# Which scores VectorE copies out of PSUM, and which two ScalarE takes as its second pair

## The chip, the core and the metric

The kernel runs on one core of a Trainium2 chip. The metric is the device time of one execution in microseconds. Engines are named as the profile names them: PE is TensorE's matmul, PEld its weight load, DVE is VectorE, ACT is ScalarE, POOL is GpSimd, SP is SyncE, which issues the DMAs.

## The reference

Two branches read the same x of 2048 rows and 512 columns, and a gate mixes them by row. Cut to what matters:

```python
# A: attention, 32 heads of 16 columns
q, k, v = split(x @ wqkv)                       # each (32, 2048, 16)
p = softmax(q @ k.T * 16**-0.5)                 # (32, 2048, 2048)
a = (p @ v) @ wo
# B: token-mixing MLP over the rows
h = layernorm(x)
b = (gelu(h.T @ w1 + b1) @ w2 + b2).T
g = sigmoid((x * gate_w).sum(-1))
out = g * a + (1 - g) * b
```

The attention has 32 x 2048 x 2048 exponentials, 134 million in all. Everything is float32; the kernel multiplies with high and low parts.

## The kernel before, in words

A first stage (to about 277 us) projects V, K and half of the queries, and runs the first layer of the MLP. Then come 128 attention *phases*, and beside them, in matmuls that use the half of PE's rows that a score leaves free, the second layer of the MLP, the late queries and the output projection ("beside" in the code, tile `dn`). A last stage finishes the output projection.

Four phases make a *group*: one pair of heads (head 0 and head 1) over half of the queries, so 32 groups. A phase computes 16 *scores*, numbered 0 to 15. A score is one matmul (L1067) of 128 keys by 512 queries, it fills one PSUM bank, and its contraction lies in the upper or the lower 64 rows of PE, by its head. In the phases with 14 matmuls beside, scores 0 to 13 are of one head, and 14 and 15, which have no matmul beside them, of one head each and run at the same time. In phases with 12 beside (16 in the middle, for late queries, and the last 16, for the output projection) 12 and 13 are of one head each too. Their order is then 12, 13, 15, 14.

Each score's exponential is taken in one of three ways:

- SINGLE: six scores, each exponentiated by ACT straight from its bank (L1093), into a tile `p`.
- TWO: two pairs of scores in neighbouring banks, a pair in one instruction of 1024 columns (L1031).
- EVAC: six scores that DVE copies (L1089) into an SBUF tile `pe`; ACT exponentiates all six at the end of the phase in one instruction of 3072 columns (L1102).

SINGLE and TWO are multiplied with V in their own phase (list TURNS), EVAC in the next one (list HELD), which the code calls held. The products (L963) are 32 columns wide and run four at a time, in four strips of PE; a pair in TURNS or HELD supplies all four. They add into one bank, `av`. In a group's first phase the held products belong to the group before and go to `av`, and the phase's own go to the bank of score 10, shown as `t`. At the end of a phase DVE adds the bank to the group's sum `ot` (L985). Which of the four quarters of the bank (two heads in column halves, two query blocks in row halves) were written decides whether that is one add of 128x512, one of 128x256, or one of 128x256 and one of 64x256.

Eight banks hold all this: one for `dn`, seven that change their use. The list `share` gives the seven banks in the order of use; scores 0 to 6 take them in that order, 7, 8 and 9 the first three again, and 10 to 15 and `av` the rest. A score must wait until the score that held its bank before was exponentiated or copied; a pair of banks is one tile (names t), released as one, and a single bank in the later part of a phase is named u.

On each engine the order is the order of the code. On DVE, work that `amid` or `between` lists for a phase stands at the last but one score, and work of `later` behind the copies.

Of the kernel before, what the change touches and what calls it, by code (L numbers as in the profile page):

```python
# [60 lines left out]
def gated_mix(ctx: ExitStack, tc: tile.TileContext, a_x, a_wqkv, a_wo, b_w1, b_b1, b_w2, b_b2, gate_w, out):  # L61
# [364 lines left out]
    with tc.tile_pool(name="gl", bufs=2, side="right") as gl:  # L426
# [74 lines left out]
        for f0, cs in order.items():  # L501
            n = min(NB, F - f0) // P
# [78 lines left out]
    PHASES, NSC, BANKS = 4, 16, 7  # L581
# [295 lines left out]
    for t in range(NS):  # L877
        at = put(second_layer(t), at, [14] * 3)
        if queries:
            b, n = queries.pop(0)  # L880
# [34 lines left out]

    token, mark = (out_pool.tile([1, 1], F32, name=name, bufs=1) for name in ("token", "mark"))

    EVAC = 1, 3, 5, 9, 14, 15
    SINGLE = 0, 2, 4, 6, 7, 8
    TWO = (10, 11), (12, 13)  # L920
    TURNS = [(0, 2), (4, 6), (7, 8), *TWO]
    HELD = [(1, 3), (5, 9), (14, 15)]

    def shares(n):

        for one in range(0, BANKS, 2):
            lows = [k for k in range(one)][::2] + [k for k in range(one + 1, BANKS)][::2]
            for third in lows:
                if n in (third, third + 1):
                    first, second = (low for low in lows if low != third)  # L930
                    return [first, first + 1, one, second, second + 1, 2 * third + 1 - n, n]


    def regions():
        return tc.tile_pool(name="ps_s", bufs=1, space=PSUM, reuse_waits="tile")
# [54 lines left out]
    with tc.manual_schedule(engines=engines):  # L990
        held, fence, turn, spare = [], None, 0, 0
        landed.clear()

        for p in range(LAST + 1):
# [22 lines left out]
            in_turn = list(range(n_b)) + ([14, 15] if n_b == NSC - 2 else [12, 13, 15, 14])  # L1017
            qbs = {}
            for a, b in TURNS + HELD:
                if head[a] == head[b]:  # L1020
# [3 lines left out]
                    qbs[zero], qbs[one] = turn, 1 - turn  # L1024
                    turn = 1 - turn

            def exps(n):
                pt = ptp.tile([P, 2, NB], F32, name="p2", bufs=len(TWO))
                where = [share[(j - BANKS) % BANKS] for j in (n - 1, n)]
                low = min(where)  # L1030
                pairs_done.append(nc.scalar.activation(pt, twos[low, low + 1], AF.Exp, scale=SCALE))  # L1031
                for j, k in zip((n - 1, n), where):
                    units[j] = *units[j][:3], pt[:, k - low, :]

            pairs_done = []
            evac = evp.tile([P, len(EVAC), NB], F32, name="pe")
            units = {}
            share = shares(spare)
# [3 lines left out]
            for n in in_turn:  # L1042
                i, qb = head[n], qbs[n]
                c = at[i][qb]
                at[i][qb] += 1
                if n < TWO[0][0]:
                    if n >= BANKS:
                        ones[share[n - BANKS]] = psum.tile([P, NB], F32, name=f"s{share[n - BANKS]}")
                    s = ones[share[n % BANKS]]
                else:  # L1050
                    if n == TWO[0][0]:
                        pool.__exit__(None, None, None)
                        pool = regions()
                        psum = pool.__enter__()
                        twos = {}
                        for low in range(BANKS):
                            if low == share[1]:
                                av = psum.tile([P, NB], F32, name="av")
                            elif low in (share[0], share[2]):
                                twos[low] = psum.tile([P, NB], F32, name=f"u{low}")  # L1060
                            elif low not in twos:
                                two = psum.tile([P, 2, NB], F32, name=f"t{low}")
                                twos[low], twos[low + 1] = two[:, 0, :], two[:, 1, :]
                                twos[low, low + 1] = two
                    s = twos[share[2 if n == NSC - 1 else (n - BANKS) % BANKS]]
                rows_i = slice(i * HALF, i * HALF + ROWS)
                nc.tensor.matmul(  # L1067
                    s,
                    kt[grp][rows_i, c * P : (c + 1) * P],
                    qt[grp][rows_i, qb * NB : (qb + 1) * NB],  # L1070
                    start=True,
                    stop=True,
                )
                if n < n_b:
                    ps, a, b, begin, last, done = beside[n]
                    mm = nc.tensor.matmul(ps, a[half], b[half], start=begin and not second, stop=last and bool(second))  # L1076
                    if n == 0 and fence is not None:
                        tc.add_manual_dep(mm.ins, fence.ins.name, SYNC, reason=REASON)
                    if n == n_b - 1:
                        fence = nc.gpsimd.memset(token, 0.0)  # L1080
                        tc.add_manual_dep(fence.ins, mm.ins.name, SYNC, reason=REASON)
                if n == in_turn[-2]:
                    if n_b and second and beside[-1][-1] in between:
                        between[beside[-1][-1]]()
                    for what, *args in amid.get(p, ()):
                        what(*args)
                if n in EVAC:
                    pt = evac[:, EVAC.index(n), :]
                    nc.vector.tensor_copy(pt, s)  # L1089
                    units[n] = i, c, qb, pt  # L1090
                elif n in SINGLE:
                    pt = ptp.tile([P, NB], F32, name="p1", bufs=len(SINGLE))
                    one = nc.scalar.activation(pt, s, AF.Exp, scale=SCALE)  # L1093
                    if n == SINGLE[-1] and p:
                        tc.add_manual_dep(one.ins, earlier.ins.name, SYNC, reason=EARLY)
                    units[n] = i, c, qb, pt
                else:
                    units[n] = i, c, qb, None
                    if n in (TWO[0][1], TWO[1][1]):
                        exps(n)  # L1100
            for x in ([evac] if p < LAST else [evac[:, :2, :], evac[:, 2:, :]]):
                done = nc.scalar.activation(x, x, AF.Exp, scale=SCALE)  # L1102
            tc.add_manual_dep(done.ins, pairs_done[0].ins.name, SYNC, reason=EARLY)
# [15 lines left out]
                what(*args)  # L1119

            turns, now_held = ([tuple(units[n] for n in pair) for pair in pairs] for pairs in (TURNS, HELD))
            spare = share[1]
            if ph == 0:
                if held:
                    apply_v(av, grp - 1, held, final=True)
                    spare = share[3]
# [103 lines left out]
    with tc.If(far_off != 0):  # L1230
        with (
# [6 lines left out]
            for b in range(ND):  # L1238
                with tc.For_i(0, P // DH, 1) as hi:
# [11 lines left out]
                    for t in range(NS):  # L1251
                        s = ps_s.tile([P, S], F32, name="s")
# [58 lines left out]
```

## Time and profile before

| | us |
|---|---|
| median of 3 runs | 1265.53 |
| lowest, highest | 1265.07, 1266.18 |
| the profiled execution | 1265.31 |
| its span from first to last instruction | 1263.5 |
| mean granted PE clock | 0.999 of full |

Read the profile by stage: a phase repeats 128 times, so a hundredth of a microsecond in each is 1.3 us in all. In the rows of the order of time, the first number is the start and the second the duration, from the start of the first to the end of the last where several equal instructions are merged (xcount). A bracket at a row's end tells how long the engine was idle before it, and what ended that. Neighbouring instructions of ACT and of DVE overlap in these rows: one starts before the other has ended.

### The profile page before, as it was taken

The numbers are of one execution on the slowest core, as the hardware profiler recorded it, in microseconds if no ns is written. First come the engines' busy times: TensorE is split into PE (matmuls) and PEld (weight loads), VectorE is DVE, ScalarE is ACT, GpSimd is POOL, SyncE is SP. The second block draws the span as 40 slices with busy tenths as digits, with TensorE's granted clock in tenths as the row PEclk, the third lists the DMA queues.
The fourth block names the chain that finished last, engine by engine and source line by source line (L and its number), as shares of the span: only waits on it lengthen the run. The fifth ranks groups of instructions, "written<-read, shape, count | busy, mean of one in ns | idle before, by whom it ended". The sixth has DMA issues, their size and how long they took to land.

```text
span 1263.5 us, 32833 instructions
## 1 busy us (share of the span) xinstructions
PE 1254.8 (99%) x13342; PEld 829.2 (66%) x13342; DVE 856.7 (68%) x1562; ACT 1069.0 (85%) x1405; POOL 198.6 (16%) x316
## 2 busy tenths in 40 slices
PE   9999999999999999999999999999999999999998
PEld 7888888875666666666666666666666666666656
DVE  5675453178767676767677677776777677678883
ACT  4443343269999999999999999999999999999990
POOL 0220444461010101010110101111111111000000
PEclk9999999999999999999999999999999999999999
DMA  4799443244744444544344433444543443366611
GB/s 134 251 340 329 143 122 106 81 127 110 214 121 104 90 102 85 158 86 97 77 105 94 99 90 83 91 87 81 113 101 73 90 100 60 56 166 175 151 60 70
DMA packets 100556, 152.32 MB, mean 121 GB/s; under 512 B 17109, under 2 KB 56171, under 8 KB 96300
## 3 DMA queue, kind: packets, MB, share of 16 engines
q1 hardware_dynamic: 99820, 149.08, 46.0%
q8 instruction: 107, 1.75, 0.6%
q10 hardware_dynamic: 576, 1.05, 0.2%
q14 instruction: 53, 0.43, 0.1%
HBM read 105.39 MB, written 44.68 MB: 119 GB/s over the span
## 4 chain that ended last, share of the span: by engine, by line
PE 96%; DVE 2%; ACT 1%; issue 0%; DVEq 0%
PE av L963 31%; PE s L1067 21%; PE acc L424 12%; PE t L1067 9%; PE acc L75 8%; PE t L963 5%; PE dn L1076 3%; PE u L1067 3%; PE pa L1162 2%; DVE pe L1089 1%; PE acc L199 1%; PE acc L268 0%; DVE ot L985 0%; PE acc L245 0%; ACT p L1093 0%; ACT pe L1102 0%
## 5 line engine op out<-in xcount | busy, mean ns | idle before, releaser
L1093 ACT ACTIVATE p<-s 128x512 f32<-128x512 f32 x768 | 411.9, 789 | 0.1
L1102 ACT ACTIVATE pe<-pe 128x3072 f32<-128x3072 f32 x129 | 380.9, 2954 | 0.0
L1067 PE MATMUL s<-qs,ks 64*128 64x512 f32 x1280 | 329.8, 400 | 0.6 <-ACT p L1093 0.6
L1089 DVE COPY pe<-s 128x512 f32<-128x512 f32 x512 | 323.6, 685 | 5.5 <-PE s L1067 1.5
L1067 PEld LDWEIGHTS s<-qs,ks 64*128 64x128 f32 x1280 | 225.7, 184 | 92.7 <-issue 52.3
L1031 ACT ACTIVATE p<-t 128x1024 f32<-128x1024 f32 x256 | 278.7, 1267 | 0.0
L963 PE MATMUL av<-p,v 128*32 128x256 f32 x3880 | 227.2, 379 | 0.0
L1089 DVE COPY pe<-u 128x512 f32<-128x512 f32 x256 | 164.8, 685 | 67.1 <-PE u L1067 67.1
L963 PE MATMUL av<-pe,v 128*32 128x256 f32 x3072 | 192.5, 383 | 0.0
L985 DVE TENSOR_TENSOR ot<-av,ot 128x512 f32<-128x512 f32 (+2 forms) x160 | 93.0, 582 | 140.9 <-PE av L963 139.6
L68 POOL TENSOR_TENSOR w_lo<-w_raw,w_hi 128x512 fp32r<-128x512 f32 (+1 forms) x128 | 153.0, 1202 | 196.8 <-ACT w_hi L67 99.9
L1076 PE MATMUL dn<-u_lo,w_hi 64*128 64x512 f32 x448 | 181.0, 404 | 0.0
L1076 PE MATMUL dn<-u_hi,w_hi 64*128 64x512 f32 x448 | 180.7, 403 | 0.0
L963 PEld LDWEIGHTS av<-p,v 128*32 128x32 f32 x3880 | 126.0, 110 | 83.3 <-ACT p L1093 0.2
L1076 PE MATMUL dn<-u_hi,w_lo 64*128 64x512 f32 x448 | 180.6, 403 | 0.0
L1067 PE MATMUL t<-qs,ks 64*128 64x512 f32 x512 | 142.5, 413 | 0.0
L963 PEld LDWEIGHTS av<-pe,v 128*32 128x32 f32 x3072 | 86.8, 109 | 80.7 <-ACT p L1093 35.7
L1080 POOL MEMSET token<- 1x1 f32 x128 | 11.3, 88 | 742.7 <-PE dn L1076 679.4
L67 ACT CAST w_hi<-w_raw 128x512 fp32r<-128x512 f32 (+1 forms) x67 | 38.0, 569 | 82.7 <-PE acc L424 63.1
L1067 PEld LDWEIGHTS t<-qs,ks 64*128 64x128 f32 x512 | 73.2, 184 | 50.8 <-ACT p L1093 48.6
L424 PE MATMUL acc<-h_hi,w_hi 128*128 128x512 f32 x224 | 87.9, 392 | 0.0
L424 PE MATMUL acc<-h_hi,w_lo 128*128 128x512 f32 x224 | 87.9, 392 | 0.0
(171 smaller groups left out, 1615.8 us busy)
## 6 DMA issues: line engine op xcount, KB each, us to landing
w_raw<-in_B_w_dram SPq DMA_DIRECT2D x96, 256.0 KB
ks<-kp SPq DMA_DIRECT2D x192, 128.0 KB
qs<-qp SPq DMA_DIRECT2D x256, 64.0 KB
kp<-pc SPq DMA_DIRECT2D x16, 512.0 KB
qp<-pc SPq DMA_DIRECT2D x8, 768.0 KB
qp<-row SPq DMA_DIRECT2D x24, 256.0 KB
v<-v SPq DMA_DIRECT2D x4, 1088.0 KB
x<-in_A_x_dram SPq DMA_DIRECT2D x16, 256.0 KB
```

The costliest lines, as they stand in the source:

```text
L67: copy(hi, src)
L68: return sub(lo, src, hi.bitcast(F32), ALU.subtract)
L75: nc.tensor.matmul(ps, a, b, start=start and n == 0, stop=stop and n == last)
L424: nc.tensor.matmul(p, a, b, start=first and k == 0, stop=last and k == 2)
L963: mm = nc.tensor.matmul(av[32 * j : 32 * (j + 1), i * QC : (i + 1) * QC], vb[b][:, v_at : v_at + 32], pt[:, h * QC : (h + 1) * QC], start= ...
L985: latest["add"] = nc.vector.tensor_tensor(x, y, x, ALU.add)
L1031: pairs_done.append(nc.scalar.activation(pt, twos[low, low + 1], AF.Exp, scale=SCALE))
L1067: nc.tensor.matmul(s, kt[grp][rows_i, c * P : (c + 1) * P], qt[grp][rows_i, qb * NB : (qb + 1) * NB], start=True, stop=True,)
L1076: mm = nc.tensor.matmul(ps, a[half], b[half], start=begin and not second, stop=last and bool(second))
L1089: nc.vector.tensor_copy(pt, s)
L1093: one = nc.scalar.activation(pt, s, AF.Exp, scale=SCALE)
L1102: done = nc.scalar.activation(x, x, AF.Exp, scale=SCALE)
```

## The change

DVE copies scores 8, 12 and 13 in place of 9, 14 and 15; score 9 becomes a single in place of 8; ACT's second pair is 14 and 15 in place of 12 and 13. So `av` takes the bank that scores 2 and 9 used, 14 and 15 the neighbouring banks of 7 and 8, and 12 and 13 get single banks. The lists TURNS and HELD follow.

```diff
-    EVAC = 1, 3, 5, 9, 14, 15
-    SINGLE = 0, 2, 4, 6, 7, 8
-    TWO = (10, 11), (12, 13)
-    TURNS = [(0, 2), (4, 6), (7, 8), *TWO]
-    HELD = [(1, 3), (5, 9), (14, 15)]
+    EVAC = 1, 3, 5, 8, 12, 13
+    SINGLE = 0, 2, 4, 6, 7, 9
+    TWO = (10, 11), (14, 15)
+    TURNS = [(0, 2), (4, 6), (7, 9), *TWO]
+    HELD = [(1, 3), (5, 8), (12, 13)]
...
-                            if low == share[1]:
+                            if low == share[2]:
                                 av = psum.tile([P, NB], F32, name="av")
-                            elif low in (share[0], share[2]):
+                            elif low in share[5:]:
                                 twos[low] = psum.tile([P, NB], F32, name=f"u{low}")
...
-                    s = twos[share[2 if n == NSC - 1 else (n - BANKS) % BANKS]]
+                    s = twos[share[(n - BANKS) % BANKS]]
...
-                    if n in (TWO[0][1], TWO[1][1]):
-                        exps(n)
+                    if n == TWO[0][1]:
+                        exps(*TWO[0])
+                    elif n == in_turn[-1]:
+                        exps(*TWO[1])
...
-            spare = share[1]
+            spare = share[2]
```

On PE, the last scores of a phase with 14 matmuls beside, before: the tile t is the pair 12 and 13, and the two u are 14 and 15; behind a row stands the engine on which it waits.

```order
L1067 MATMUL t_8628<-qs,ks 128x512 [waits DVE_49,Activation_49]
L1076 MATMUL dn<-u_hi,w_hi 128x512
L1067 MATMUL t_8628<-qs,ks 128x512
L1076 MATMUL dn<-u_lo,w_hi 128x512
L1067 MATMUL u_8629<-qs,ks 128x512 [waits Activation_49]
L1067 MATMUL u_8627<-qs,ks 128x512 [waits DVE_49]
L963 MATMUL av<-pe,v_113 32x256 [waits Activation_49]
```

The same place after:

```order
L1067 MATMUL u_8634<-qs,ks 128x512 [waits DVE_49]
L1076 MATMUL dn<-u_hi,w_hi 128x512
L1067 MATMUL u_8633<-qs,ks 128x512 [waits Activation_49]
L1076 MATMUL dn<-u_lo,w_hi 128x512
L1067 MATMUL t_8636<-qs,ks 128x512 [waits DVE_49,Activation_49]
L1067 MATMUL t_8636<-qs,ks 128x512
L963 MATMUL av<-pe,v_113 32x256 [waits Activation_49]
```

The pair now comes last, and its first matmul waits both for DVE's copy of score 8 and for ACT's single of score 7; scores 12 and 13 wait for one engine each.

On DVE, from the end of a group's first phase to the copies of its second, before: the first two adds are of the held products, the third of the phase's own (t), then come the copies.

```order
L985 TENSOR_TENSOR ot<-av,ot 128x256
L985 TENSOR_TENSOR ot<-av,ot 64x256
L985 TENSOR_TENSOR ot<-t_8631,ot 128x256
L1089 COPY pe<-s_8711 128x512
L1089 COPY pe<-s_8712 128x512
L1089 COPY pe<-s_8715 128x512
L1089 COPY pe<-s_8751 128x512
```

The same place after:

```order
L985 TENSOR_TENSOR ot<-av,ot 128x256
L985 TENSOR_TENSOR ot<-av,ot 64x256
L985 TENSOR_TENSOR ot<-t_8637,ot 128x256
L985 TENSOR_TENSOR ot<-t_8637,ot 64x256
L1089 COPY pe<-s_8718 128x512
L1089 COPY pe<-s_8719 128x512
L1089 COPY pe<-s_8722 128x512
L1089 COPY pe<-s_8753 128x512
```

A second add of the phase's own products, 64x256, now stands ahead of the copies. In groups that follow a phase with 14 matmuls beside, the 64x256 add of the held products is gone in return.

More of the change, by code (lines that the diff above doesn't have):

```diff
@@ L1025, in gated_mix, with exps @@
                     turn = 1 - turn
-            def exps(n):
+            def exps(a, b):
                 pt = ptp.tile([P, 2, NB], F32, name="p2", bufs=len(TWO))
-                where = [share[(j - BANKS) % BANKS] for j in (n - 1, n)]
+                where = [share[(j - BANKS) % BANKS] for j in (a, b)]
                 low = min(where)
                 pairs_done.append(nc.scalar.activation(pt, twos[low, low + 1], AF.Exp, scale=SCALE))
-                for j, k in zip((n - 1, n), where):
+                for j, k in zip((a, b), where):
                     units[j] = *units[j][:3], pt[:, k - low, :]
```

## The prediction

> **What bounds the kernel now.** I read the page first, then the waits, then the order of time engine by engine through one group of four attention phases. The page says PE 99% and puts nearly the whole chain on PE:
>
> ```profile
> span 1263.5 us, 32833 instructions
> PE 1254.8 (99%) x13342; PEld 829.2 (66%) x13342; DVE 856.7 (68%) x1562; ACT 1069.0 (85%) x1405; POOL 198.6 (16%) x316
> PE 96%; DVE 2%; ACT 1%; issue 0%; DVEq 0%
> ```
>
> The 85% of ACT is a mean over stages. The 128 attention phases run from its first exponential at 278.1 us to its last at 1227.4, and there ACT has no idle time; behind its rows stand the busy times of an ordinary group and of one of the last four (PE, PEld, DVE, ACT, POOL):
>
> ```profile
> L1093 ACT ACTIVATE p<-s x768: 579/801/871, 278.1 to 1224.2; 128x512 f32<-128x512 f32 x192
> L1102 ACT ACTIVATE pe<-pe x129: 1177/3001/3020, 283.0 to 1227.4; 128x3072 f32<-128x3072 f32 x127, 128x1024 f32<-128x1024 f32 x1, 128x2048 f32<-128x2048 f32 x1
> ...
> 604.90:634.60 29.70, 29.69 (x376) 18.04 (x372) 21.94 (x40) 29.70 (x37) 2.17 (x6) 1.00 0.41 92
> 1109.40:1139.30 29.90, 29.79 (x374) 18.19 (x370) 23.98 (x45) 29.90 (x37) 0.88 (x5) 1.00 0.70 177
> ```
>
> PE and ACT are both full, so the order of time must tell which sets the pace. ACT, in order: six singles (scores exponentiated straight from PSUM, L1093), two pairs (L1031), the big exponential of the six copied scores (L1102), the next singles:
>
> ```profile
> 602.79 3.00 ACT L1102 ACTIVATE pe<-pe 128x3072 f32<-128x3072 f32 x1
> 605.49 3.24 ACT L1093 ACTIVATE p<-s 128x512 f32<-128x512 f32 x6
> 608.37 2.19 ACT L1031 ACTIVATE p<-t 128x1024 f32<-128x1024 f32 x2
> 610.21 3.00 ACT L1102 ACTIVATE pe<-pe 128x3072 f32<-128x3072 f32 x1
> 612.90 3.24 ACT L1093 ACTIVATE p<-s 128x512 f32<-128x512 f32 x6
> ```
>
> Each row begins before the one ahead of it has ended: the singles at 605.49, the big exponential ahead at 605.79, an overlap of 0.30 us. So starts say little; I read the ends: 605.79, 608.73 (+2.94), 610.56 (+1.83), 613.21 (+2.65), together 7.42. Compare a place where the big exponential had started late and the overlap was small:
>
> ```profile
> 862.73 2.77 ACT L1102 ACTIVATE pe<-pe 128x3072 f32<-128x3072 f32 x1
> 865.40 3.02 ACT L1093 ACTIVATE p<-s 128x512 f32<-128x512 f32 x6
> 868.26 1.99 ACT L1031 ACTIVATE p<-t 128x1024 f32<-128x1024 f32 x2
> 870.07 2.84 ACT L1102 ACTIVATE pe<-pe 128x3072 f32<-128x3072 f32 x1
> ```
>
> Here the overlap is 0.10 (865.50 less 865.40), and the ends still stand +2.92, +1.83 and +2.66 apart: 7.41. So ACT's work, counted from end to end, takes 7.42 us a phase whether its instructions start early or late, and a start may come 0.20 us later than it does now (0.30 less 0.10) before an end moves. That is the cushion of this kernel.
>
> PE is tied to it. PE's weight loads: the phase's first score, its last two scores, the first product with V, the next phase's first score:
>
> ```profile
> 604.95 0.18 PEld L1067 LDWEIGHTS s<-qs,ks 64*128 64x128 f32 x1 [0.41 <-issue]
> 608.29 0.19 PEld L1067 LDWEIGHTS u<-qs,ks 64*128 64x128 f32 x2 [0.19 <-ACT p L1093]
> 608.78 1.02 PEld L963 LDWEIGHTS av<-pe,v 128*32 128x32 f32 x24 [0.30 <-ACT p L1093]
> 612.37 0.18 PEld L1067 LDWEIGHTS s<-qs,ks 64*128 64x128 f32 x1 [0.41 <-issue]
> 634.63 0.18 PEld L1067 LDWEIGHTS s<-qs,ks 64*128 64x128 f32 x1 [0.41 <-issue]
> ```
>
> The products start at 608.78, 0.05 after the last single ended (608.73), because av takes that single's bank. From there to the next phase is 3.59 us of products. So a phase is 7.42, the group 604.95 to 634.63 is 29.68, and ACT's ends set both.
>
> **The change part by part.**
>
> *The wait ahead of the big exponential goes.* Now DVE copies scores 14 and 15 last:
>
> ```profile
> 605.72 2.52 DVE L1089 COPY pe<-s 128x512 f32<-128x512 f32 x4
> 608.83 1.29 DVE L1089 COPY pe<-u 128x512 f32<-128x512 f32 x2 [0.58 <-PE u L1067]
> ```
>
> They end at 610.12 and the exponential starts at 610.21, 1.84 after the first pair; at 868.26, where nothing held it, it took 1.81. So 0.03 us a phase of waiting, 128 x 0.03 = 3.8 us if it counted. With the copies of 12 and 13 following that of 8 at 0.61 us each (2.52 over four, less the last one's tail), six copies end near 609.5, and that wait is over. I cost the gain at nothing: an earlier start only adds to an overlap of 0.30 that is already larger than the 0.10 ACT needs. Bounds: 0 and -3.8 us.
>
> *The second pair now waits for the last two scores.* Those matmuls start with the load at 608.29 and take about 0.5 (the row at 1120.50 below), so they are there by 608.8; the second pair starts 0.92 after 608.37 (half of 1.84), at 609.29. Margin 0.5 us: nothing. The last products use this pair last of 64 matmuls, over 2 us later. av moves to the bank of score 9, again the phase's last single, so its release stays at 608.73. Scores 14 and 15 now need both the single of 7 (the wait in the row at 608.29 today) and DVE's fourth copy, which is of score 8 instead of 9: the same place in DVE's order, ended at 608.24. Nothing.
>
> *The sums' adds move.* Which quarters of av were written decides how DVE adds them (L985). The scores on two heads were 14 and 15, held over; now they are in TURNS, so in all groups the first phase's own products fill three quarters, not two, and need a 128x256 and a 64x256 add. Today that is so in the last four groups alone:
>
> ```profile
> L985 DVE TENSOR_TENSOR ot<-av,ot x160: 402/690/693, 284.1 to 1231.4; 128x512 f32<-128x512 f32 x95, 128x256 f32<-128x256 f32 x34, 64x256 f32<-64x256 f32 x31
> L985 DVE TENSOR_TENSOR ot<-t,ot x35: 423/425/427, 315.9 to 1206.9; 128x256 f32<-128x256 f32 x31, 64x256 f32<-64x256 f32 x4
> ```
>
> The 4 becomes 31 (27 more); in return 64x256 adds of the held products fall away in the middle of a phase, where DVE waits for PE anyway. The new adds stand right ahead of the second phase's copies. What that does is seen in the last four groups (DVE, then PE's loads, a last-scores matmul, and ACT):
>
> ```profile
> 1117.07 0.87 DVE L985 TENSOR_TENSOR ot<-t,ot 128x256 f32<-128x256 f32 x2 [1.33 <-issue]
> 1117.96 2.48 DVE L1089 COPY pe<-s 128x512 f32<-128x512 f32 x4
> 1121.04 1.29 DVE L1089 COPY pe<-u 128x512 f32<-128x512 f32 x2 [0.59 <-PE u L1067]
> ...
> 1109.45 0.18 PEld L1067 LDWEIGHTS s<-qs,ks 64*128 64x128 f32 x1 [0.41 <-issue]
> 1116.87 0.18 PEld L1067 LDWEIGHTS s<-qs,ks 64*128 64x128 f32 x1 [0.41 <-issue]
> 1120.50 0.19 PEld L1067 LDWEIGHTS u<-qs,ks 64*128 64x128 f32 x2 [0.32 <-DVE pe L1089]
> 1124.52 0.18 PEld L1067 LDWEIGHTS s<-qs,ks 64*128 64x128 f32 x1 [0.41 <-issue]
> 1131.91 0.18 PEld L1067 LDWEIGHTS s<-qs,ks 64*128 64x128 f32 x1 [0.41 <-issue]
> 1139.26 0.18 PEld L1067 LDWEIGHTS s<-qs,ks 64*128 64x128 f32 x1 [0.41 <-issue]
> ...
> 1120.50 0.50 PE L1067 MATMUL u<-qs,ks 64*128 64x512 f32 x2
> ...
> 1121.19 1.29 ACT L1031 ACTIVATE p<-t 128x1024 f32<-128x1024 f32 x1
> 1122.42 2.77 ACT L1102 ACTIVATE pe<-pe 128x3072 f32<-128x3072 f32 x1
> ```
>
> The copies begin 1.09 after the phase's first score, against 0.77 (605.72 less 604.95). The fourth ends at 1120.44, and only then (1120.50) can the last scores be loaded; the phase lasts 1116.87 to 1124.52, 7.65 us, 0.23 more than 7.42. So in 27 more groups PE comes 0.23 late to the third phase's first score. ACT's single then starts 0.23 later; the cushion takes 0.20. I cost 0.03 x 27 = +0.8 us. The cushion must be refilled in the three other phases: PE, when ACT does not hold it, takes 7.39 and 7.35 (1124.52, 1131.91, 1139.26) against ACT's 7.42, and slightly less once the fourth copy need not wait for score 9 (2.48 against 2.52): near 0.07 a phase, 0.2 in three. Just enough. Bounds: 0, if the refill is ample; 0.13 a group, 3.5 us, if such a group becomes what the last four are now (29.81, from 1109.45 to 1139.26, against 29.68). I take 0.03, since those four pay for something the change removes, the next point.
>
> *The last four groups.* There the late last scores also delay their copies (1121.04) and with them the big exponential: 1122.42, 1.23 after its pair at 1121.19, against 0.92. After the change copies 12 and 13 do not come behind the last scores, and the pair's scores are there at 1121.00, before 1121.19. These groups fall from 29.81 to the others' 29.68 + 0.03: 4 x -0.10 = -0.4 us.
>
> Sum: +0.8 - 0.4 = +0.4 us on the profiled execution's 1265.31, which lies 0.2 under the median of 1265.53; on the median, **1265.9 us**.
>
> **The rivals.**
>
> *Slower: the cushion does not hold.* Mechanism: the added 64x256 add makes the third phase's first score late. If groups come out as the last four now, 27 x 0.13 = 3.5 us, 1269.0; if nothing is absorbed, 27 x 0.23 = 6.2 us, 1271.7. It decides from 0.11 us a group on (2.5 + 0.4 over 27). For it: the refill is barely enough. Against it: at 862.73 the overlap fell to 0.10 and ACT's ends kept their distance. The Trainium skill (ScalarE: Activation LUTs, What ACT_TABLE_LOAD costs) says that ACTIVATEs back to back overlap by about 93 ns, which would leave no cushion and make it the 1271.7; the trace agrees with 0.10 as the least overlap, but shows 0.30 as the usual one.
>
> *Faster: ACT's pace is that of its starts.* Singles start 0.48 apart (2.88 over six), and the big exponential's 0.03 of wait per phase would then be real: -3.8 us, 1261.7. Against it: the ends' distance is the same with and without waits, and PE's products go by an end. The Trainium skill (Perfetto Trace Analysis, Optimizing Scalar/DVE Operations) gives about 51 ns per ScalarE instruction on PSUM and 93 on SBUF; with the 0.833 ns an element of its ScalarE page that is an estimate of 7.32 us a phase, so that ACT would have idle time to give; the starts agree with it, the ends (7.42) do not.
>
> **How the numbers follow.** Unchanged within 0.2% (2.5 us, about what a measurement of this kernel can tell from no change): 0.74. The cushion does not hold: 0.20 (0.12 near 1269.0, 0.08 above). Faster: 0.06. The range: ACT's lost time in the last groups won back with no cost elsewhere is 1265.1, and 0.6 for the scatter of runs (1265.07 to 1266.18) gives 1264.5 below; above it reaches to 1269.0, the last four groups' price everywhere.
>
> **What would show it.** Right: adds ot<-t of 64x256 number 31; second phases of 7.6 to 7.7 in all groups; the last copies end some 0.6 before the big exponential; ACT's ends stay 7.42 apart, a group 29.7. Wrong: a group of 29.8 or more in the middle, with singles starting less than 0.1 before the exponential ahead ends; or phases under 7.40 throughout, which would mean that the ends' pace was not ACT's own.

## The result, and the profile after

The changed kernel takes 1275.16 us (median of 4 runs, 1274.51 to 1275.29), the kernel before beside it 1265.84 (4 runs): the ratio is 1.0074, with a 95% interval of 1.0062 to 1.0086. So it is 9.3 us slower, where no change was forecast (1265.9, at most 1269.0). The profiled execution took 1275.29 us; its span is 10.0 us longer than before's 1263.5.

The page of the changed kernel: its span, the busy times, the chain that ended last by engine, and two groups of instructions (busy time, mean ns of one, idle time ahead of them).

```profile
span 1273.5 us, 32694 instructions
PE 1261.1 (99%) x13342; PEld 844.3 (66%) x13342; DVE 859.7 (68%) x1570; ACT 1072.2 (84%) x1405; POOL 198.6 (16%) x316
PE 91%; ACT 5%; DVE 3%; issue 1%; DVEq 0%
L1093 ACT ACTIVATE p<-s 128x512 f32<-128x512 f32 x768 | 391.1, 624 | 6.7 <-PE s L1067 6.6
L1089 DVE COPY pe<-u 128x512 f32<-128x512 f32 x256 | 164.9, 686 | 5.6 <-PE dn L1076 1.6
```

The same two groups before:

```profile
L1093 ACT ACTIVATE p<-s 128x512 f32<-128x512 f32 x768 | 411.9, 789 | 0.1
L1089 DVE COPY pe<-u 128x512 f32<-128x512 f32 x256 | 164.8, 685 | 67.1 <-PE u L1067 67.1
```

Two things are new. ACT's singles, which were never late, now wait 6.6 us for PE's scores. And the last copies of a phase, which waited 67.1 us for PE before, wait 5.6. The shorter mean of a single (624 ns, 789 before) is not a faster ACT: an instruction that begins early behind its neighbour shows a longer duration, so the short mean says that ACT's lead over its own ends is gone.

The order of time says where the 10 us are. First, PE's weight loads from group to group: the first score of each of the four phases, the last two scores (now the pair t) and the next group's first score.

```profile
578.48 0.18 PEld L1067 LDWEIGHTS s<-qs,ks 64*128 64x128 f32 x1 [0.41 <-issue]
...
585.91 0.18 PEld L1067 LDWEIGHTS s<-qs,ks 64*128 64x128 f32 x1 [0.41 <-issue]
...
593.65 0.18 PEld L1067 LDWEIGHTS s<-qs,ks 64*128 64x128 f32 x1 [0.41 <-issue]
...
601.09 0.18 PEld L1067 LDWEIGHTS s<-qs,ks 64*128 64x128 f32 x1 [0.41 <-issue]
...
604.46 0.22 PEld L1067 LDWEIGHTS t<-qs,ks 64*128 64x128 f32 x2 [0.30 <-ACT p L1093]
604.92 1.02 PEld L963 LDWEIGHTS av<-pe,v 128*32 128x32 f32 x24 [0.24 <-ACT p L1093]
...
608.51 0.18 PEld L1067 LDWEIGHTS s<-qs,ks 64*128 64x128 f32 x1 [0.41 <-issue]
```

The phases last 7.43, 7.74, 7.44 and 7.42, the group 30.03 where it was 29.68. All of the loss is in the second phase, and nothing of it comes back in the other three. 27 groups at about 0.33 are 8.9 us. The last four, which stood at 29.81 before, take the same 29.99 now (1118.52 to 1148.51, from one group's first score to the next one's), 0.7 us more; together 9.6.

DVE in the second phase and in the fourth (adds, copies of 1, 3, 5 and 8, copies of 12 and 13):

```profile
586.10 0.87 DVE L985 TENSOR_TENSOR ot<-t,ot 128x256 f32<-128x256 f32 x2 [1.33 <-issue]
587.00 2.48 DVE L1089 COPY pe<-s 128x512 f32<-128x512 f32 x4
589.48 1.29 DVE L1089 COPY pe<-u 128x512 f32<-128x512 f32 x2
...
601.86 2.48 DVE L1089 COPY pe<-s 128x512 f32<-128x512 f32 x4
604.37 1.29 DVE L1089 COPY pe<-u 128x512 f32<-128x512 f32 x2
```

The copies start 1.09 after the phase's first score in the second phase, 0.77 in the fourth: the second add costs 0.32, as forecast from the old last groups (1.09 against 0.77), and as forecast it is there in all groups:

```profile
L985 DVE TENSOR_TENSOR ot<-t,ot x62: 424/426/430, 316.1 to 1216.6; 128x256 f32<-128x256 f32 x31, 64x256 f32<-64x256 f32 x31
```

ACT through the same stretch:

```profile
591.12 2.84 ACT L1104 ACTIVATE pe<-pe 128x3072 f32<-128x3072 f32 x1
594.19 3.05 ACT L1093 ACTIVATE p<-s 128x512 f32<-128x512 f32 x6 [0.23 <-PE s L1067]
...
598.88 2.84 ACT L1104 ACTIVATE pe<-pe 128x3072 f32<-128x3072 f32 x1
601.62 3.05 ACT L1093 ACTIVATE p<-s 128x512 f32<-128x512 f32 x6
...
606.31 2.84 ACT L1104 ACTIVATE pe<-pe 128x3072 f32<-128x3072 f32 x1
609.05 1.08 ACT L1093 ACTIVATE p<-s 128x512 f32<-128x512 f32 x2
```

The big exponential ends at 593.96 and the third phase's singles start 0.23 later, because its score is not there yet. From there the singles begin 0.10 before the exponential's end (601.62 against 601.72, 609.05 against 609.15), the least that was seen before, and no more: the cushion is empty and is never refilled. Yet ACT no longer holds PE: the last single of the fourth phase ends at 604.67 (601.62 and 3.05), and the products start at 604.92, 0.25 later, where they followed the single by 0.05 before. So in these phases PE takes 7.42 or 7.43 of its own, where 7.39 and 7.35 were expected of it. PE's way through the fourth phase goes over DVE: 0.77 from the first score to the copies, 2.48 for the four copies, 0.12 to the loads of the last two scores, 0.46 from there to the products and 3.59 of products, 7.42 in all. Of these it is the 0.12 that has grown. The copy of 8 ends at 604.34 (601.86 and 2.48), and the loads of 14 and 15 come 0.12 behind it, at 604.46. Before, they came 0.05 behind the fourth copy (608.24 and 608.29). The line of the scores, asked for that moment alone (604.3 to 608), shows what stands between:

```profile
L1067 PEldq EVENT_SEMAPHORE  x1: 51/51/51, 604.4 to 604.4; - x1
```

One of the two waits is an instruction of its own, 51 ns long, on PE's sequencer (PEldq). It runs only when the copy has ended, so it is the one that waits for DVE, the later of the two engines, and the load comes behind it. The Trainium skill (Perfetto Trace Analysis, Identifying Dependency Chains) says that an instruction that waits on several engines may have such instructions put ahead of it; the trace agrees, and adds the price.

The change hardly adds such instructions: the line of the scores has 304 of them, and had 297 before. It moves them. Before, the two-engine wait of a phase's last four scores stood on score 12: its instruction, at 607.6, was over before the load at 607.80, which came behind an exponential of ACT. Now it stands on score 14, right behind the copy that PE waits for.

### The profile page after: what moved, and what is told of

It reads as the page before. It is cut to its first block, busy times and chain, and to the rows that moved or that the text cites. A ratio compares the mean times of both kernels' runs of the same rounds, so it can differ in the third digit from the quotient of the medians.

```text
span 1273.5 us, 32694 instructions
## 1 busy us (share of the span) xinstructions
PE 1261.1 (99%) x13342; PEld 844.3 (66%) x13342; DVE 859.7 (68%) x1570; ACT 1072.2 (84%) x1405; POOL 198.6 (16%) x316
## 4 chain that ended last, share of the span: by engine, by line
PE 91%; ACT 5%; DVE 3%; issue 1%; DVEq 0%
PE av L963 29%; PE s L1067 18%; PE acc L424 12%; PE acc L75 8%; PE t L1067 7%; PE dn L1076 5%; PE t L963 5%; PE u L1067 3%; ACT p L1093 2%; DVE pe L1089 2%; ACT pe L1104 2%; PE pa L1164 2%; PE acc L199 1%; DVE ot L985 1%; PE acc L268 1%
## 5 line engine op out<-in xcount | busy, mean ns | idle before, releaser
L1093 ACT ACTIVATE p<-s 128x512 f32<-128x512 f32 x768 | 391.1, 624 | 6.7 <-PE s L1067 6.6
L1104 ACT ACTIVATE pe<-pe 128x3072 f32<-128x3072 f32 x129 | 364.6, 2828 | 0.0
L1089 DVE COPY pe<-s 128x512 f32<-128x512 f32 x512 | 318.2, 683 | 1.0
L1067 PEld LDWEIGHTS s<-qs,ks 64*128 64x128 f32 x1280 | 222.6, 184 | 93.6 <-issue 52.3
L1031 ACT ACTIVATE p<-t 128x1024 f32<-128x1024 f32 x256 | 257.4, 1101 | 0.0
L985 DVE TENSOR_TENSOR ot<-av,ot 128x512 f32<-128x512 f32 (+2 forms) x141 | 85.2, 605 | 198.9 <-PE av L963 198.4
L1067 PE MATMUL t<-qs,ks 64*128 64x512 f32 x512 | 145.9, 440 | 4.5 <-DVE pe L1089 1.4
```

The costliest lines, as they stand in the source:

```text
L985: latest["add"] = nc.vector.tensor_tensor(x, y, x, ALU.add)
L1067: nc.tensor.matmul(s, kt[grp][rows_i, c * P : (c + 1) * P], qt[grp][rows_i, qb * NB : (qb + 1) * NB], start=True, stop=True,)
```

## The experiments

Two theories were to be told apart first. One (two-wait theory): the added add is passed on whole because the two-engine wait takes the slack from the path over PE and DVE in every phase. The other (add-alone theory): the add costs its 0.33 us in any case. A third (order theory), that the new order of singles and pairs costs the time itself, was kept beside them. Times are medians, beside 1265.50 us (first four kernels) and 1265.55 us (last four) of the kernel before.

**The changed kernel without the second add.** It leaves out that quarter of a group's first-phase sums.

```diff
-            at += [(rows[qb], cols[i]) for i, qb in sorted(met) if (i, 1 - qb) not in met]
+            at += [(rows[qb], cols[i]) for i, qb in sorted(met) if final and (i, 1 - qb) not in met]
```

> The changed kernel without the 64x256 add of a first phase's own products, so that no add stands ahead of the second phase's copies a second time; it leaves out that quarter of the sums. Two-wait theory (the add's 0.33 us is passed on whole because the first matmul of score 14 waits for two engines, which costs the path over TensorE and VectorE 0.06 to 0.09 us in every phase and leaves nothing to refill ScalarE's lead): every phase at 7.41 to 7.43 us, 1263 to 1266 us. Add-alone theory (the add costs 0.33 us in 31 groups whatever the wait): 1263 to 1266 us too. Order theory (the new order of singles and pairs costs the time itself, and the add is beside it): it stays at 1273 to 1275 us.

Measured: 1264.14 us, ratio 0.9989 (0.9980 to 0.9998). The order theory is out: with the new order and without the add, nothing is lost. It is even 1.4 us under the kernel before; 4 x 0.13, some 0.5, is what the last groups paid for their second add. The rest is not accounted for, but it is not in the other groups: those 27 take 29.67 on average in both traces (309.02 to 1110.20 here, 308.24 to 1109.45 before).

**The kernel before with a second add.**

```diff
             at += [(rows[qb], cols[i]) for i, qb in sorted(met) if (i, 1 - qb) not in met]
+            if not final and len(met) == 2:
+                at = [(rows[qb], cols[i]) for i, qb in sorted(met)]
```

> The kernel before with the first phase's own 128x256 add made as two adds of 64x256, so that two adds stand ahead of the second phase's copies in 31 groups and not only in the last four, while score 14 and score 15 keep one wait each. Two-wait theory: these groups go like the last four groups of the kernel before, 29.80 us and not 29.67, so 27 x 0.13 = 3.5 us more, 1268 to 1270 us. Add-alone theory: 27 x 0.33 = 8.9 us more, 1273 to 1276 us. Order theory: no change, 1265 to 1266.5 us.

Measured: 1266.95 us, ratio 1.0012 (1.0002 to 1.0021), 1.45 us more: 0.05 in each of 27 groups, less than either theory gave. The add alone does not cost 0.33 a group. A group's phases, the second one from 583.37 on:

```profile
576.01 0.18 PEld L1069 LDWEIGHTS s<-qs,ks 64*128 64x128 f32 x1 [0.41 <-issue]
...
583.37 0.18 PEld L1069 LDWEIGHTS s<-qs,ks 64*128 64x128 f32 x1 [0.41 <-issue]
...
591.01 0.18 PEld L1069 LDWEIGHTS s<-qs,ks 64*128 64x128 f32 x1 [0.41 <-issue]
...
605.76 0.18 PEld L1069 LDWEIGHTS s<-qs,ks 64*128 64x128 f32 x1 [0.41 <-issue]
```

The second phase takes 7.64, the first 7.36, and the other two 14.75 together: what the second loses, the others win back but for 0.07.

**The kernel before with 8 and 9 exchanged**, as in the change, and nothing else. Scores 14 and 15 then follow the single of 7 and the copy of 8, as in the change, but in banks of their own and with one wait each.

```diff
-    EVAC = 1, 3, 5, 9, 14, 15
-    SINGLE = 0, 2, 4, 6, 7, 8
+    EVAC = 1, 3, 5, 8, 14, 15
+    SINGLE = 0, 2, 4, 6, 7, 9
```

(TURNS, HELD and the bank of av follow.)

> The kernel before with scores 8 and 9 exchanged alone: VectorE copies 8, 14 and 15 out, ScalarE's last single is that of 9, and the pairs stay 10 with 11 and 12 with 13. No add moves and score 14 keeps one wait. All three theories: 1264.5 to 1266.5 us; over 1268 us would speak against all of them.

Measured: 1265.39 us, ratio 1.0001 (0.9992 to 1.0010). No change; ACT's ends hold the pace.

**The kernel before with the two-engine wait.**

```diff
+                    for prior in (9, 7):
+                        tc.add_manual_dep(score.ins, copied[prior].ins.name, SYNC, reason=EARLY)
```

(for the first of the last two scores; copied holds the instruction that copied or exponentiated a score)

> The kernel before, in which the first of the last two scores' matmuls is made to wait both for VectorE's fourth copy and for ScalarE's single of 7, as in the changed kernel; nothing else is changed. Two-wait theory: the second wait makes a row of its own on TensorE's queue and the matmul's weight load starts some 0.06 us later behind the copy; phases of 7.42 us that TensorE paces grow to 7.45 or more: 0.03 to 0.06 us in 124 phases, 4 to 7 us more, 1269 to 1273 us. Add-alone and order theories: no change, 1265 to 1266.5 us.

Measured: 1270.93 us, ratio 1.0042 (1.0028 to 1.0056). The wait alone costs 5.4 us, as the two-wait theory said. The line of the scores has 424 semaphore rows where the kernel before had 297, one more for nearly every phase; first the kernel before, then this one:

```profile
L1067 PEldq EVENT_SEMAPHORE  x297: 51/51/51, 274.7 to 1223.9; - x149
```

```profile
L1067 PEldq EVENT_SEMAPHORE  x424: 51/51/51, 274.5 to 1229.6; - x142
```

And its phases are longer than the 7.42 that ACT needs, two of them 14.91:

```profile
576.36 0.18 PEld L1067 LDWEIGHTS s<-qs,ks 64*128 64x128 f32 x1 [0.41 <-issue]
...
591.27 0.18 PEld L1067 LDWEIGHTS s<-qs,ks 64*128 64x128 f32 x1 [0.41 <-issue]
```

So both parts have a price of their own, 1.45 and 5.4, and their sum, 6.9, is not the change's 9.3. Moreover, in the change the wait follows the copy of 8, which ends earlier than that of 9, so that its own price should be less than 5.4. The question became whether the two add up (sum theory) or act on one another (interaction theory): the add's delay has to be refilled from slack that the wait spends. Four kernels answered it, three of which take the kernel with 8 and 9 exchanged and add the wait, the add, and both.

**With the wait** (on the copy of 8 and the single of 7):

```diff
+                    for prior in (8, 7):
+                        tc.add_manual_dep(score.ins, copied[prior].ins.name, SYNC, reason=EARLY)
```

> The kernel before with scores 8 and 9 exchanged (1265.39 us) and, on top of it, the first of the last two matmuls made to wait for two engines, VectorE's copy of 8 and ScalarE's single of 7, as in the changed kernel. No add moves. Interaction theory (the two-engine wait lifts TensorE's own way through a phase from about 7.35 to 7.42 us, which is just ScalarE's 7.42, so by itself it costs nothing but takes the slack away): phases of 7.42 us with ScalarE's overlap going down slowly, 1264.5 to 1266.5 us. Sum theory (each part has a price of its own: the wait 5.4 us as measured with the copy of 9): 1268 to 1271 us.

Measured: 1266.73 us, ratio 1.0010 (1.0001 to 1.0019), 1.2 us more than the kernel before, and 0.2 over what the interaction theory allowed. Three phases of its middle, 582.93 to 605.19, and one of the last groups:

```profile
582.93 0.18 PEld L1067 LDWEIGHTS s<-qs,ks 64*128 64x128 f32 x1 [0.41 <-issue]
...
605.19 0.18 PEld L1067 LDWEIGHTS s<-qs,ks 64*128 64x128 f32 x1 [0.41 <-issue]
...
1109.80 0.18 PEld L1067 LDWEIGHTS s<-qs,ks 64*128 64x128 f32 x1 [0.41 <-issue]
...
1139.79 0.18 PEld L1067 LDWEIGHTS s<-qs,ks 64*128 64x128 f32 x1 [0.41 <-issue]
```

The three phases take 22.26, 7.42 each. In the middle the wait is almost free. In the last groups, which have their second add by nature, it is not: 29.99 (1109.80 to 1139.79) against before's 29.81, and that is 0.7 of the 1.2 us.

**With the second add:** the edit of the second experiment.

> The kernel before with scores 8 and 9 exchanged and the first phase's own add split in two, so that a second add stands ahead of the second phase's copies in 31 groups; score 14 and score 15 keep one wait each. Interaction theory: second phases of about 7.6 us, the others about 7.35 where ScalarE does not hold them, so that its lead is refilled and the group stays within 0.05 us of before: 1265 to 1267 us. Sum theory: 1266 to 1267.5 us as well (the split add cost 1.45 us on the kernel before).

Measured: 1265.58 us, ratio 1.0000 (0.9991 to 1.0009). The add, alone, costs nothing that can be told from zero. ACT in this kernel shows the cushion at work:

```profile
580.85 2.98 ACT L1104 ACTIVATE pe<-pe 128x3072 f32<-128x3072 f32 x1
583.53 3.24 ACT L1095 ACTIVATE p<-s 128x512 f32<-128x512 f32 x6
...
588.47 2.79 ACT L1104 ACTIVATE pe<-pe 128x3072 f32<-128x3072 f32 x1
591.17 3.05 ACT L1095 ACTIVATE p<-s 128x512 f32<-128x512 f32 x6
...
595.86 2.83 ACT L1104 ACTIVATE pe<-pe 128x3072 f32<-128x3072 f32 x1
598.51 3.12 ACT L1095 ACTIVATE p<-s 128x512 f32<-128x512 f32 x6
...
603.19 2.93 ACT L1104 ACTIVATE pe<-pe 128x3072 f32<-128x3072 f32 x1
605.84 0.76 ACT L1095 ACTIVATE p<-s 128x512 f32<-128x512 f32 x1
```

Singles begin 0.30 before the big exponential's end, then 0.09 after the second phase, then 0.18, then 0.28. The exponentials' ends stand 7.43 apart throughout (583.83, 591.26, 598.69, 606.12). The singles' starts stand 7.64, 7.34 and 7.33 apart.

**With both:** the two edits above together.

> Both at once, on the kernel before with scores 8 and 9 exchanged: the add split in two and the two-engine wait on score 14. Copies of 12 and 13 and the new place of ScalarE's second pair, the rest of the change, are not in it. Interaction theory: the changed kernel's loss comes back whole: second phases of 7.72 to 7.76 us, the other three 7.41 to 7.43, 1273 to 1276 us. Sum theory: what the two cost singly, 1265.5 + 1.5 + at most 5.4, 1267 to 1272.5 us. Order theory (the pair's new place is needed for the loss): 1265 to 1268 us.

Measured: 1274.57 us, ratio 1.0070 (1.0056 to 1.0084), 9.0 us more than the kernel before. Singly the two cost 1.2 and 0.0; together 9.0. This is the change's loss, without its new copies and without its new place of the pair. The phases, second, third and fourth:

```profile
585.77 0.18 PEld L1069 LDWEIGHTS s<-qs,ks 64*128 64x128 f32 x1 [0.41 <-issue]
...
593.50 0.18 PEld L1069 LDWEIGHTS s<-qs,ks 64*128 64x128 f32 x1 [0.41 <-issue]
...
596.87 0.21 PEld L1069 LDWEIGHTS u<-qs,ks 64*128 64x128 f32 x2 [0.27 <-ACT p L1097]
597.32 1.02 PEld L963 LDWEIGHTS av<-pe,v 128*32 128x32 f32 x24 [0.24 <-ACT p L1097]
...
600.91 0.18 PEld L1069 LDWEIGHTS s<-qs,ks 64*128 64x128 f32 x1 [0.41 <-issue]
...
608.32 0.18 PEld L1069 LDWEIGHTS s<-qs,ks 64*128 64x128 f32 x1 [0.41 <-issue]
```

They last 7.73, 7.41 and 7.41. The third phase of the kernel with the add alone, for comparison:

```profile
590.64 0.18 PEld L1069 LDWEIGHTS s<-qs,ks 64*128 64x128 f32 x1 [0.41 <-issue]
...
593.77 0.34 PEld L1069 LDWEIGHTS u<-qs,ks 64*128 64x128 f32 x2
594.36 1.02 PEld L963 LDWEIGHTS av<-pe,v 128*32 128x32 f32 x24 [0.24 <-ACT p L1095]
...
597.95 0.18 PEld L1069 LDWEIGHTS s<-qs,ks 64*128 64x128 f32 x1 [0.41 <-issue]
```

It lasts 7.31. DVE's fourth copy ends 3.24 after the first score's load in both (the four copies, of the add alone and then of both):

```profile
591.40 2.48 DVE L1091 COPY pe<-s 128x512 f32<-128x512 f32 x4
```

```profile
594.26 2.48 DVE L1093 COPY pe<-s 128x512 f32<-128x512 f32 x4
```

That is at 593.88 and at 596.74. The first product is loaded 0.48 behind it with one wait each, and 0.58 behind it with two. Of these 0.10 us, some 0.07 are the semaphore instruction: the load behind the copy comes 0.12 or 0.13 after it instead of 0.05 (the second of the two loads of 0.34, which takes 0.18 and ends at 594.11, starts at 593.93). The other 0.03 is score 14: with one wait its load went ahead of the copy's end (593.77), with two it stands between the copy and the load of 15.

Now all of these kernels come out, nearly, by one rule: a group takes PE's own way or ACT's, whichever is longer. ACT's is 4 x 7.42 = 29.68. PE's is added up from the phases shown; the fourth column is the mean of the 27 ordinary groups in the trace, 29.67 in the kernel before.

| kernel | PE's own way in a group | over 29.68 | mean group | us measured over before |
|---|---|---|---|---|
| 8 for 9, second add | 7.64 + 3 x 7.31 = 29.57 | none | 29.71 | 0.0 |
| 8 for 9, wait | 4 x 7.42 = 29.68 | none | 29.68 | 1.2 (0.7 of it in the last groups) |
| 8 for 9, both | 7.73 + 3 x 7.41 = 29.96 | 0.28 | 29.99 | 9.0 |
| before, second add | 7.64 + 7.36 + 14.75 = 29.75 | 0.07 | 29.77 | 1.45 |
| before, wait (on the copy of 9) | 2 x 14.91 = 29.82 | 0.14 | 29.83 | 5.4 |
| the change | 7.43 + 7.74 + 7.44 + 7.42 = 30.03 | 0.35 | 30.00 | 9.3 |

Only the first row forecasts a group from phases of which some were held by ACT, and there it is 0.03 too short. In the last four rows PE's way is the measured group itself; what shows that it is PE's is that the products start 0.11 to 0.57 behind the last single there (medians by phase), and 0.05 behind it in the kernel before, where ACT holds them. The third column times 27, and the last four groups on top, comes within 0.9 us of the measured loss. With the wait on the copy of 9 the last groups take 30.09 (1113.37 to 1143.46, again first scores' loads), 0.28 over before: 27 x 0.14 and 4 x 0.28 make 4.9 of the 5.4.

**The changed kernel with the old order in a group's first phase.** Here the first phase copies 9, 14 and 15 and the three others 8, 12 and 13, so that the second add is not needed outside the last four groups, and all is computed.

```diff
+            EVAC, SINGLE, TWO, TURNS, HELD = orders(ph == 0)
...
-                            if low == share[2]:
+                            if low == share[1 if ph == 0 else 2]:
```

(orders gives the lists of before or of the change)

> The changed kernel with the lists of the kernel before in a group's first phase alone, so that this phase's own products fill two quarters of the sums and need one add; the other three phases copy 8, 12 and 13 and have the two-engine wait. All is computed. Interaction theory: without the second add nothing has to be refilled, all phases 7.41 to 7.43 us: 1263.5 to 1266 us, at or just under the kernel before. Sum theory: three quarters of the wait's price stay, 1268 to 1270 us. Order theory: 1271 to 1273 us.

Measured: 1265.07 us, ratio 0.9997 (0.9987 to 1.0006). The change in three quarters of the phases, with its two-engine wait, costs nothing once the add is not there. The same trace shows the other case: the last groups, which have the add, take 29.96 (1109.10 to 1139.06). The kernel is not measurably faster than the kernel before either: ACT's 7.42 a phase stays. No kernel that computes everything was clearly faster than the kernel before.

Not tried: the changed order with one wait on the pair. The pair is one tile whose two banks were freed by two engines. What that order would be worth without the second wait stays open.

## Why the prediction was wrong

Point by point:

- **ACT's ends set the pace, with a cushion of 0.20.** Right for the kernel before. In the kernel with 8 for 9 and the second add the overlap goes from 0.30 to 0.09 and back while the ends keep 7.43.
- **The wait ahead of the big exponential goes, and gains nothing.** Right, as far as shown: without the second add the 27 groups take 29.67, as before. The last copies end 0.65 before it in the fourth phase (605.66 against 606.31; 0.6 was said) and 0.35 before it in the second.
- **The second pair waits for the last two scores: nothing.** Half wrong, and this is the step that failed: "Scores 14 and 15 now need both the single of 7 [...] and DVE's fourth copy, which is of score 8 instead of 9: the same place in DVE's order, ended at 608.24. Nothing." The pair itself is in time: in the fourth phase its matmuls end at 604.99, and ACT begins it near 605.4, 0.9 after the first pair. But I asked only when the last of the two engines was done, and not what it costs PE to wait for two: 0.10 us a phase, 0.07 for an instruction of its own and 0.03 for a load that can no longer go ahead. The semaphore rows of 51 ns were in the trace of the kernel before (297 of them, on other scores), and the order of the code, known beforehand, has the two-engine wait move to score 14; the price could have been bounded from there.
- **The adds move.** Right in number (31 rows) and place. The second phase was said to take 7.65, from the old last groups; it takes 7.74, those 7.65 and the wait's 0.09.
- **The cushion must be refilled: "near 0.07 a phase, 0.2 in three. Just enough."** Right for PE's way without the second wait: with 8 for 9 and the add, the time is that of before (1265.58). With the wait nothing is left of it: PE takes 7.42 in the other phases, as much as ACT, and 0.33 of 0.33 goes into the end. The term was +0.8 us and measures 8.9.
- **The last four groups fall by 0.4 us.** Wrong by the same wait: they went from 29.81 to 29.99, +0.7.
- **The rival "the cushion does not hold"**, which had a chance of 0.20, is what happened. Its price, 27 x 0.23 = 6.2 at the most, was short of 8.9, since it too used phases of 7.65 against 7.42 and left the wait out. With the measured terms the sum is 1265.31 + 8.9 + 0.7 = 1274.9, against 1275.29 of the profiled execution.
- **The rival "ACT's pace is that of its starts"** is out: with 8 for 9 and the second add, starts 7.64, 7.34 and 7.33 apart go with ends 7.43 apart each time. Starts that near the estimate of 7.32 appear only while the lead is refilled. The Trainium skill (ScalarE: Activation LUTs, What ACT_TABLE_LOAD costs) gives an overlap of about 93 ns for ACTIVATEs back to back; the traces agree for an ACT without a lead (0.10 in the changed kernel), and with a lead show three times that (0.30).

## What to carry to other kernels

Where two engines take nearly the same time for a repeated unit, write down each one's own way through that unit and take the longer: an edit that costs the second engine 0.1 us is free up to the point where the two are level, and from there on every further cost is paid whole. In this program a matmul into a tile whose parts were freed by two engines waits in two steps; look at which of the two releases comes last and what lies behind it, and if it is on the path, keep the parts on one engine or in tiles of their own. And before saying that a slack refills, check that nothing else in the same edit spends it.

## What the runs showed of the hardware

- A second engine to wait for, when it is the later one, costs PE 51 ns for a semaphore instruction, and the load then starts 0.12 to 0.13 us behind the release instead of 0.05. Where ACT holds the pace, the time hardly shows it: with 8 for 9 and the wait the 27 groups take 29.68 on average, and 29.67 before.
- The durations of ACT's neighbouring instructions hold its lead in them. A single showed 789 ns on average in the kernel before and 624 in the changed one, while the big exponential's ends stood 7.42 us apart before and 7.43 in the changed kernel's fourth phase.
